# Turning two more tiles with VectorE, and moving turns and splits within their steps, in a two-layer linear-attention and MLP kernel

## The chip, the cores and the metric

The kernel runs on one core of a Trainium2 chip. A core has five engines with a queue each: TensorE (PE in the profile, with its weight loads as PEld), VectorE (DVE), ScalarE (ACT), GpSimd (POOL) and SyncE (SP). Each works through its own instructions in the order in which they were issued; semaphores make one wait for another. Here SP issues nearly all DMAs, so its queue is the order of the transfers. The metric is the device time of one execution in microseconds.

## The reference

The input x has 2048 rows of 448 numbers, all in float32. Two layers are applied, with the same weights. Each is a linear attention block (16 heads of 28) followed by an MLP with a hidden width of 1792:

```
phi = lambda t: where(t > 0, t + 1, exp(t)) + 1e-6
for layer in range(2):
    q, k, v = split(layernorm(x) @ wqkv)
    kv  = einsum("bhsd,bhse->bhde", phi(k), v)
    z   = phi(k) summed over the rows
    o   = (phi(q) @ kv) / (phi(q) . z + 1e-6)        # per head
    x   = x + o @ wo
    x   = x + gelu(layernorm(x) @ w1 + b1) @ w2 + b2
```

## The kernel before, in words

**Precision.** A float32 product is made of three products of halves: every operand is split into a high part (a cast) and a low part (the rest). hi x hi, hi x lo and lo x hi are accumulated in PSUM. A cast on ScalarE makes the high part, and VectorE or GpSimd subtracts to get the low part.

**Phase 1 of a layer** runs over 16 tiles of 128 rows, one step per tile. Around step t TensorE does, in this order: the K product of tile t (`proj`, L337, 11 matmuls of 128x448 into `psk`), the transposes of tile t+1 where TensorE makes them (L262, four into `tp`), the G product of tile t-1 (`stage_g`, L592, 11 matmuls, which gather phi(k) times x) and, in steps 2 to 8 of layer 0, the Q product of tile t (L337, `psq`). Of layer 0's other Q products, two are made ahead of the steps and seven behind them. From step 9 on a step has no Q product.

**Two ways to transpose.** K and Q need the normalised tile with its columns on the partitions, split into `XH` and `XL`. Way one: TensorE transposes into PSUM (`stage_b`), ScalarE casts from there (L274) and VectorE subtracts (L275). For the odd 64 columns at the end of such a tile ScalarE first copies them twice (L430, into spare space in `b2b`). Way two, the "turned" tiles: VectorE transposes in blocks of 32 (`turn`, L301 and L302) into half of a square `sq`; when the second tile of a pair is done, SP stores the square to DRAM (L307), and four DMAs bring it back spread as wanted (`spread`, L313, into `sp`). Then ScalarE casts from `sp` to `XH` (L319) and VectorE subtracts, from SBUF (`split_t`, L320). `TURNED` holds the first turned tile of each layer: 8 in layer 0, so tiles 0 to 7 go the first way there; in layer 1 all are turned.

**The order of a step** is written out by hand as tokens, in `STEP` for most steps and `STEPS` for others. Every engine gets its instructions in that order:

- `qp`: phi of the last Q product: two ScalarE activations (L353, L354), one VectorE operation (L356), and the store of the result to DRAM by SP (L565)
- `K`, `T`, `G`, `Q`: TensorE's products and the transposes of tile t+1
- `X`: the split of tile t+1 into `XH` and `XL` (ScalarE, then VectorE)
- `s`: the split of the normalised tile t for G (ScalarE cast L461; GpSimd L462 and L463)
- `a`, `aN`: layer norm's statistics of tile N (VectorE L207, L219, L212), and the power -0.5 on GpSimd (L213)
- `n`, `nN`: the normalisation of tile N (VectorE L426), which needs that power
- `kp`, `kh`, `kl`: phi of K (ScalarE, then VectorE L356), its high part (ScalarE L501), its low part and the running sum `za` (VectorE L510, L517)
- `tu`, `vN`: the turn of a tile, and the store if it ends a pair
- `bg`: in layer 0, the MLP's weights: SP loads pieces (L101 to L104, L392), and of pieces loaded earlier ScalarE casts the high part (L384, L387, L395) and GpSimd makes the low part (L385, L388, L396), up to two pieces a step until step 7, one later
- `ld`: SP loads later tiles of x (L85); `sp`: SP issues the spreads of all squares stored so far

The plain `a`, `n` and `tu` take their tile from `NORM`. Its row for step 5 is tile 10, for step 6 tile 11, for step 7 tile 12 and for step 8 tile 13.

The squares, the spread tiles and some weight pieces share five buffers of 128x1024, given out in turn. `k_at`, `q_at` and `g_at` say at which places among the 11 matmuls of a product those stand that read a low part of the tile: (2, 5, 8, 11) in K means that the second matmul already reads `XL`.

**Behind phase 1** a short transition forms the 448x448 matrix of the attention, and four MLP blocks of four tiles follow.

Of the kernel before, what the change touches and what calls it, by code (L numbers as in the profile page):

```python
# [22 lines left out]
def linear_attn_mlp_kernel(  # L23
# [12 lines left out]
    pe, act, dve, pool, sp = nc.tensor, nc.scalar, nc.vector, nc.gpsimd, nc.sync  # L36
# [8 lines left out]
    G = 112  # L45
# [37 lines left out]
    def load_x(l, t):  # L83
        xt[l, t] = t448("H", 8, f"x{l}_{t}")
        sp.dma_start(xt[l, t], x_d[l][t * 128:(t + 1) * 128, :])  # L85
# [164 lines left out]
    def block(key):  # L250
        if key not in blocks:
            blocks[key] = Block(APART if key[0] == "a" else 0)
        return blocks[key]
# [3 lines left out]
    def transpose_x(xn, tail, key, j, tag="m"):  # L257

        block(key)
        tp = tps[key, j] = bank(tag, 4 if tag == "acc" else 2, "tp")  # L260
        for c in range(4):
            pe.transpose(tp[:, c * 128:(c + 1) * 128], xn[:, c * 128:(c + 1) * 128] if c < 3 else tail, ident)  # L262
# [8 lines left out]
    def split_x(key, j):  # L271
        tp = tps.pop((key, j))
        hi, lo = blocks[key].pieces(j)
        act.copy(hi, tp)  # L274
        dve.tensor_sub(lo, tp, f(hi))  # L275
# [20 lines left out]
    def turn(x, key, t):  # L296
        x = x[:, :D]
        if (key, t // 2) not in squares:
            squares[key, t // 2] = half("sq")
        sq = squares[key, t // 2].rearrange("p (m c u n) -> p c m u n", m=4, c=4, n=32)[:, :, :, t % 2]  # L300
        dve.transpose(sq[:, :3], x[:, :TL].rearrange("p (c m n) -> p c m n", c=3, n=32))  # L301
        dve.transpose(sq[:, 3].rearrange("p (u m) n -> p u m n", u=2),  # L302
                      x[:, TL:].rearrange("p (m n) -> p m n", n=32)[:, None].to_broadcast([128, 2, 2, 32]))
# [56 lines left out]
    def bg_pieces():  # L360
        n = 0
        both = []

        def stage():
            nonlocal n
            n += 1
            if n <= LATE:
                k = (n - 1) // 2
                if k % 2 == 0 or k > 5:
                    return t512("xn", 2, "stg")[:, :D]  # L370

                if n % 2:
                    both.append(half("stg"))
                return both[-1][:, n % 2 * 512:][:, :D]
            return t448(f"W{5 + n % 2}", 1, "stg")

        for fc in range(4):
            sl = slice(fc * D, (fc + 1) * D)
            for c in range(4):
                s = stage_piece(w1[:, sl], c, sp, stage())  # L380

                def go(c=c, s=s, sl=sl):
                    if c < 3:
                        act.copy(w1h[:, c, sl], s)  # L384
                        pool.tensor_tensor(w1l[:, c, sl], s, f(w1h[:, c, sl]), op=OP.subtract)  # L385
                    else:
                        act.copy(w1x[:, sl], s)  # L387
                        pool.tensor_tensor(w1x[64:128, sl], s[64:128], f(w1x[64:128, sl]), op=OP.subtract)  # L388
                yield go
        for i in range(NF):  # L390
            s = stage()
            sp.dma_start(s, w2[i * 128:(i + 1) * 128, :])  # L392

            def go(i=i, s=s):
                act.copy(w2h[:, i], s)  # L395
                pool.tensor_tensor(w2l[:, i], s, f(w2h[:, i]), op=OP.subtract)  # L396
            yield go

    bg = bg_pieces()
# [14 lines left out]
    sts = {}  # L414


    TURNED = (8, 0)
    tails = {}

    def stage_a(l, t):  # L420
# [2 lines left out]
    def stage_n(l, t):  # L423
# [3 lines left out]
        xns[l, t] = xs  # L427
        if t < TURNED[l]:
            d = tails[l, t] = b2b[:, t % 2 * 128:][:, :128]
            act.copy(d.rearrange("p (u n) -> p u n", u=2), xs[:, None, TL:].to_broadcast([128, 2, 64]))  # L430

    def stage_t(l, t):
        if t >= TURNED[l]:
            turn(xns[l, t], ("a", l, t // 4), t % 4)
            if t % 2:
                store_sq(("a", l, t // 4), t % 4 // 2)

    def stage_sp(l, t):
        if t >= TURNED[l]:
            block(("a", l, t // 4))  # L440
            spread(("a", l, t // 4), t % 4 // 2)

    def stage_b(l, t, tag="h"):
        if t < TURNED[l]:
            transpose_x(xns[l, t], tails.pop((l, t)), ("a", l, t // 4), t % 4, tag)
# [4 lines left out]
    def stage_x(l, t):  # L450
        key = ("a", l, t // 4)
        if t < TURNED[l]:
            split_x(key, t % 4)
# [13 lines left out]

    def k_at(l, t):
        if t < 9:
            return (3, 6, 9, 11) if t == 0 or l == 0 and 2 < t < 8 else (2, 5, 8, 11)  # L470
        return (2, 5, 8, 11) if t == 9 else (1, 4, 7, 10)

    def q_at(l, t):
        if t < 9:
            return (2, 5, 8, 11) if l == 0 and t < 7 else (2, 4, 7, 10) if t == 0 else (1, 4, 7, 10)
        return {11: (4, 7, 10, 11), 12: (5, 7, 9, 11),
                13: (5, 8, 10, 11), 15: (1, 5, 8, 11)}.get(t, (1, 4, 7, 10))

    def g_at(l, t):
        if t < 9:  # L480
            return (4, 7, 10) if l == 0 and 0 < t < 6 else (3, 6, 9)
        return (2, 5, 8) if t < NT - 1 else (2, 6, 9)

    def stage_k(l, t, cs=range(4)):
        ko[l, t] = proj("k", ("a", l, t // 4), t % 4, ko.get((l, t)), cs, k_at(l, t))
# [47 lines left out]
    def stage_q(l, t, cs=range(4), tag=None):  # L533
        if tag:
            qs_[l, t] = bank(tag, 4, "psq")[:, :D]
        qs_[l, t] = proj("q", ("a", l, t // 4), t % 4, qs_.get((l, t)), cs, q_at(l, t))
        if 3 in cs:
            qo.append((l, t, qs_.pop((l, t))))
# [19 lines left out]
    def stage_qphi(n=9):  # L558
        for _ in qo[:n]:
            l, t, o = qo.pop(0)  # L560
            if (l, t) == (0, 0):
                by_rs(o)

            e = phi(o, "eq", tag="e" if t < NT - 2 else "E")
            sp.dma_start(pq_d[l][t * 128:(t + 1) * 128, :], e)  # L565

    def fill_qphi():

        l, t, o = qo.pop(0)
        e = t512("e", 3, "eq")[:, :D]  # L570
        p = t512("E", 2, "ep")[:, :D]
        act.activation(e, o, AF.Relu, scale=-1.0)
        act.activation(p, o, AF.Relu)
        act.activation(e, e, AF.Exp, scale=-1.0)
        pool.tensor_tensor(e, p, e, op=OP.add)
        sp.dma_start(pq_d[l][t * 128:(t + 1) * 128, :], e)

    def stage_g(l, t, acc, mid=lambda: None):
        h, lo = split.pop((l, t))
        kh, kl = ks.pop((l, t))  # L580
        first, last = t == 0, t == NT - 1
        x = [h[:, c * 128:(c + 1) * 128] for c in range(3)] + [h[:, TL:]]
        his = [(c, x[c], k) for c in range(4) for k in (kh, kl)]
        if t == NT - 3:
            his = his[::2] + his[1::2]
        los = [(c, lo[:, c * 128:(c + 1) * 128], kh) for c in range(3)]
        made = merge(his, los, g_at(l, t))
        for i, (c, w, k) in enumerate(made):
            if i == 3:
                mid()  # L590
            others = [m[0] for m in made[:i]], [m[0] for m in made[i + 1:]]
            pe.matmul(acc[c], w, k, start=first and c not in others[0], stop=last and c not in others[1])  # L592
# [20 lines left out]
    STEPS = {  # L613
# [9 lines left out]
    }  # L623
# [123 lines left out]
    def trans_gt(tr, acc):  # L747
        tr.gt = []
        for c in range(4):
            s = t512("A" if c < 2 else "B", 2, "gt")[:, :D]  # L750
            act.copy(s, acc[c])
            tr.gt.append(s)
# [52 lines left out]
    def load_pq(l, b, j):  # L805
        t = b * 4 + j
        pqt[l, t] = t448(f"W{j}", 1, f"pq{l}_{t}")
        sp.dma_start(pqt[l, t], pq_d[l][t * 128:(t + 1) * 128, :])
# [259 lines left out]
    for l in range(LAYERS):  # L1068
# [11 lines left out]
        def pre(j):  # L1080
# [6 lines left out]
            Q=lambda j: stage_q(l, fill.pop(0)), Qp=lambda j: fill_qphi(), Qv=lambda j: stage_qphi(j or 9),  # L1087
            Qa=lambda j: stage_q(l, fill.pop(0), tag="acc"), G=lambda j: stage_g(l, NT - 1, acc, lambda: trans_z(tr, zs[l])),
            ld=lambda j: (load_pq(l, 0, j), load_x(l, j)), gt=lambda j: trans_gt(tr, acc),
# [14 lines left out]
        for b in range(NB):  # L1104
# [6 lines left out]
            for i in range(NF):  # L1111
# [12 lines left out]
                elif l + 1 < LAYERS:  # L1124
# [4 lines left out]
                    if i in (3, 4, 6, 7, 8):  # L1129
                        t = (3, 4, 6, 7, 8).index(i)  # L1130
# [36 lines left out]
```

## Time and profile before

| | |
|---|---|
| median of 3 runs | 867.03 us (866.88 to 867.56) |
| the profiled execution | 866.72 us, its span 865.0 us |
| TensorE busy | 860.0 us, 99% of the span |
| VectorE, ScalarE, GpSimd busy | 57%, 40%, 24% |
| layer 0, step 3 (26.25 to 33.42) | VectorE 5.96 of 7.17 us |
| layer 0, step 4 (33.42 to 40.47) | VectorE 6.33 of 7.05 us |
| layer 0, step 5 (40.47 to 47.52) | VectorE 6.79 of 7.05 us |
| layer 0, step 8 (61.19 to 67.79) | VectorE 5.11 of 6.60 us |

A row of a timeline gives the start of an instruction from the span's start, its duration, engine, line, operation, what it writes and reads with shapes, and, where the engine was idle just before it, for how long and what ended that. Rows of one engine can overlap by some hundredths of a microsecond up to a tenth, because an instruction begins while the last one drains; so the pace of an engine is the difference of two starts. The matmul rows are pipelined as well, which is why the view of the chain, where pieces are joined end to end, is used for TensorE. Of step t, "start" is the start of its K product. SPq rows are the issues of DMAs.

### The profile page before, as it was taken

To read this page: it belongs to the slowest core of one execution; us is meant where nothing else is said; L and a number is where in the kernel's file an instruction comes from. 1 tells how busy PE (TensorE), PEld (TensorE's weight loads), DVE (VectorE), ACT (ScalarE), POOL (GpSimd) and SP (SyncE) were. 2 spreads that over 40 slices of the span, in tenths; PEclk is the share of its full clock that TensorE was granted. 3 is DMA by queue.
4 is the path that set the end of the run, shared out by engine and by line. 5 is a ranking of instruction groups with operands and counts; after the bars stand their busy time and mean duration, and the time that the engine had idled before them with its cause. 6 is when DMAs were issued, how large, how long until landed. Compare 5 with 4: busy or idle time off the path is not lost.

```text
span 865.0 us, 11662 instructions
## 1 busy us (share of the span) xinstructions
PE 860.0 (99%) x4181; PEld 770.6 (89%) x4181; DVE 494.6 (57%) x966; ACT 346.5 (40%) x606; POOL 211.1 (24%) x243
## 2 busy tenths in 40 slices
PE   9999999999999999999999999999999999999998
PEld 8999988888888888888899998988888888888887
DVE  7888596559456443236477876864674383533112
ACT  7776635333323322333356565433232233233231
POOL 3665612235013012012222343120220140140000
PEclk9999999999999999999999999999999999999999
DMA  5385536533313402051145433252332413111001
GB/s 171 128 248 174 183 90 216 183 112 108 134 61 117 147 0 98 1 182 49 49 152 185 163 130 108 103 187 80 117 109 88 139 72 112 50 49 43 0 1 43
DMA packets 63642, 94.76 MB, mean 110 GB/s; under 512 B 8928, under 2 KB 58720, under 8 KB 63584
## 3 DMA queue, kind: packets, MB, share of 16 engines
q1 hardware_dynamic: 63408, 93.87, 33.0%
q8 instruction: 33, 0.54, 0.3%
q14 instruction: 25, 0.20, 0.1%
q10 hardware_dynamic: 176, 0.14, 0.0%
HBM read 56.17 MB, written 34.60 MB: 105 GB/s over the span
## 4 chain that ended last, share of the span: by engine, by line
PE 99%; DVE 0%; issue 0%; ACT 0%; DVEq 0%
PE hp L924 32%; PE y L954 10%; PE y L953 10%; PE y L955 10%; PE G L592 8%; PE psq L337 8%; PE psk L337 8%; PE op L862 2%; PE op L861 2%; PE op L863 2%; PE op L851 1%; PE op L850 1%; PE op L852 1%; PE kvp L759 1%; PE mp L769 1%; PE psk L551 1%
## 5 line engine op out<-in xcount | busy, mean ns | idle before, releaser
L930 DVE TENSOR_TENSOR gl<-g,gh 128x512 fp32r<-128x512 f32 x112 | 83.2, 743 | 293.8 <-ACT gh L929 293.8
L926 ACT ACTIVATE g<-hp,b1s 128x512 f32<-128x512 f32 x112 | 77.4, 691 | 399.6 <-PE hp L924 398.8
L954 PE MATMUL y<-w2l,gh 128*128 128x448 f32 x447 | 163.6, 366 | 0.0
L953 PE MATMUL y<-w2h,gh 128*128 128x448 f32 x447 | 162.0, 362 | 0.0
L955 PE MATMUL y<-w2h,gl 128*128 128x448 f32 x447 | 160.1, 358 | 0.0
L924 PE MATMUL hp<-XH,w1h 128*128 128x512 f32 x336 | 130.7, 389 | 0.0
L924 PE MATMUL hp<-XH,w1l 128*128 128x512 f32 x336 | 130.7, 389 | 0.0
L924 PE MATMUL hp<-XL,w1h 128*128 128x512 f32 x336 | 130.1, 389 | 0.0
L213 POOL TENSOR_TENSOR brs<-bve,mhalf 128x1 f32<-128x1 f32 x63 | 39.3, 623 | 286.0 <-DVE bve L212 285.5
L953 PEld LDWEIGHTS y<-w2h,gh 128*128 128x128 f32 x447 | 83.7, 187 | 9.4
L954 PEld LDWEIGHTS y<-w2l,gh 128*128 128x128 f32 x447 | 83.9, 188 | 7.0
L955 PEld LDWEIGHTS y<-w2h,gl 128*128 128x128 f32 x447 | 84.0, 188 | 5.2 <-DVE gl L930 0.2
L924 PEld LDWEIGHTS hp<-XL,w1h 128*128 128x128 f32 x336 | 63.1, 188 | 13.1
L924 PEld LDWEIGHTS hp<-XH,w1h 128*128 128x128 f32 x336 | 63.0, 187 | 10.7
L924 PEld LDWEIGHTS hp<-XH,w1l 128*128 128x128 f32 x336 | 63.1, 188 | 9.9
L929 ACT CAST gh<-g 128x512 fp32r<-128x512 f32 x112 | 70.1, 626 | 3.5
L337 PE MATMUL psk<-wk,XH 128*128 128x448 f32 x210 | 61.8, 364 | 0.0
L337 PE MATMUL psq<-wq,XH 128*128 128x448 f32 x210 | 61.3, 366 | 0.0
L812 POOL TENSOR_TENSOR pz<-pq,zb 128x448 f32<-128x448 f32 x32 | 36.9, 1154 | 90.5 <-DVE dn L818 59.1
L462 POOL TENSOR_TENSOR xnl<-x,xnh 128x384 fp32r<-128x384 f32 x32 | 34.8, 1088 | 70.0 <-ACT xnh L461 56.7
L592 PE MATMUL G<-kh,xnh 128*128 128x448 f32 x128 | 46.8, 368 | 0.0
L592 PE MATMUL G<-kl,xnh 128*128 128x448 f32 x128 | 46.0, 365 | 0.0
(161 smaller groups left out, 1481.7 us busy)
## 6 DMA issues: line engine op xcount, KB each, us to landing
x<-in_A_x_dram SPq DMA_DIRECT2D x32, 224.0 KB, 3.7
pq_d<-eq SPq DMA_DIRECT2D x32, 224.0 KB, 2.7
pq<-pq_d SPq DMA_DIRECT2D x32, 224.0 KB, 3.2
sq_m<-sq SPq DMA_DIRECT2D x14, 512.0 KB, 2.8
sp<-sq_m SPq DMA_DIRECT2D x56, 128.0 KB, 2.8
x<-x_d SPq DMA_DIRECT2D x32, 224.0 KB, 3.5
sq_a<-sq SPq DMA_DIRECT2D x12, 512.0 KB, 2.9
sp<-sq_a SPq DMA_DIRECT2D x48, 128.0 KB, 2.8
```

The lines of the kernel that those rows point to most:

```text
L213: pool.tensor_tensor(rs, ve, mhalf, op=OP.pow)
L337: pe.matmul(o, x, p, start=(i == 0), stop=(i == 10))
L462: pool.tensor_tensor(lo[:, :TL], xn[:, :TL], f(h[:, :TL]), op=OP.subtract)
L592: pe.matmul(acc[c], w, k, start=first and c not in others[0], stop=last and c not in others[1])
L812: pool.tensor_tensor(pz, pqt[l, b * 4 + j], tr.zb, op=OP.mult)
L924: pe.matmul(o, w, r, start=(k == 0), stop=(k == len(made) - 1))
L926: act.activation(g, hp, AF.Gelu_apprx_tanh, bias=b1s[:, i:i + 1])
L929: act.copy(gh, g)
L930: dve.tensor_sub(gl, g, f(gh))
L953: pe.matmul(acc[j], gh[:, s], w2h[:, i], start=first, stop=False)
L954: pe.matmul(acc[j], gh[:, s], w2l[:, i], start=False, stop=False)
L955: pe.matmul(acc[j], gl[:, s], w2h[:, i], start=False, stop=stop)
```

## The change

In layer 0 tiles 6 and 7 are turned as well, so the tiles from 6 on take the way through `sq` and `sp`. Their turns stand in step 3. Step 3 loses the statistics of tile 8 and gets the normalisations of 6 and 7 (6 alone before); step 4 does the statistics of 8 and 9, the normalisation of 8 and the turn of 8; the normalisation and the turn of 9 stand at the head of step 5, and the turns of 10 to 14 at the head of steps 6 to 10 rather than late in steps 5 to 9. In steps 5 to 8, X stands behind kl rather than ahead of s; in step 5 the normalisation of 10 stands behind X. The tokens for spreads move with the stores: they stand at the end of steps 3, 5, 7, 9 and 10 (4, 6, 8 and 10 held work before). The places of the low matmuls in K, Q and G change for a few tiles.

```diff
-    TURNED = (8, 0)
+    TURNED = (6, 0)
...
     def k_at(l, t):
         if t < 9:
-            return (3, 6, 9, 11) if t == 0 or l == 0 and 2 < t < 8 else (2, 5, 8, 11)
+            return (3, 6, 9, 11) if t == 0 or l == 0 and 2 < t < 6 else (2, 5, 8, 11)
         return (2, 5, 8, 11) if t == 9 else (1, 4, 7, 10)
 
     def q_at(l, t):
         if t < 9:
-            return (2, 5, 8, 11) if l == 0 and t < 7 else (2, 4, 7, 10) if t == 0 else (1, 4, 7, 10)
+            return (2, 5, 8, 11) if l == 0 and t < 5 else (2, 4, 7, 10) if t == 0 else (1, 4, 7, 10)
...
     def g_at(l, t):
         if t < 9:
-            return (4, 7, 10) if l == 0 and 0 < t < 6 else (3, 6, 9)
+            return (4, 7, 10) if l == 0 and 0 < t < 4 else (3, 6, 9)
...
     STEPS = {
         (0, 1): "T X a3 q1 s kh n3 kl q1 G bg ld",
         (0, 2): "K T X s a4 kp n4 a5 kh kl n5 a6 G bg Q ld",
-        (0, 3): "qp K T X s a7 kp kh n6 kl a8 G bg Q ld",
-        (0, 4): "qp K T X s a9 kp kh n7 n8 kl n9 v8 v9 G bg Q ld sp",
-        (0, 8): "qp K T X s a kp n kh kl tu a14 G bg Q ld sp",
-        (0, 9): "qp K T X s kp n14 kh kl v14 G bg",
-        (0, 10): "K T X s a15 kp n15 kh kl v15 G bg sp",
+        (0, 3): "qp K T X n6 s a7 kp kh n7 v6 v7 kl G bg Q ld sp",
+        (0, 4): "qp K T X s a8 kp kh n8 a9 kl v8 G bg Q ld",
+        (0, 5): "qp K n9 v9 s a10 kp kh kl X n10 G bg Q ld sp",
+        (0, 6): "qp v10 K s a11 kp n11 kh kl X G bg Q ld",
+        (0, 7): "qp v11 K s a12 kp n12 kh kl X G bg Q ld sp",
+        (0, 8): "qp v12 K s a13 kp n13 kh kl X a14 G bg Q ld",
+        (0, 9): "qp v13 K X s kp n14 kh kl G bg sp",
+        (0, 10): "K v14 X s a15 kp n15 kh kl v15 G bg sp",
         (0, 11): "K T X kp s kh kl G bg",
         (1, 0): "K T X s kp kh kl a n tu Q ld sp",
     }
```

The steps without an entry of their own (5, 6 and 7 of layer 0 before) follow `STEP = "qp K T X s a kp n kh kl tu G bg Q ld sp"`.

## The prediction

> **What bounds the kernel now.** I read the page's busy shares and its chain first, then the chain in order of time for the first 220 us, and then the timelines of ScalarE (ACT), VectorE (DVE) and GpSimd (POOL) around the steps that change.
>
> ```profile
> span 865.0 us, 11662 instructions
> PE 860.0 (99%) x4181; PEld 770.6 (89%) x4181; DVE 494.6 (57%) x966; ACT 346.5 (40%) x606; POOL 211.1 (24%) x243
> ...
> PE 99%; DVE 0%; issue 0%; ACT 0%; DVEq 0%
> ```
>
> TensorE is the chain, so only two things move the end: matmul time taken away, and waits put into TensorE's stream. Step 4 of layer 0 and the start of step 9, in the chain's order (start, us, what):
>
> ```profile
> 33.42 2.21 PE psk L337 x11
> 35.63 0.44 PE tp L262 x4
> 36.06 2.21 PE G L592 x11
> 38.27 2.20 PE psq L337 x11
> ...
> 67.79 2.20 PE psk L337 x11
> ```
>
> A step is the K product (2.21 us), the next tile's four transposes (0.44), the G product of the tile before (2.21) and the Q product (2.20), with no gap: 7.06 us, or 6.61 without transposes. One matmul is 2.2 / 11 = 0.20.
>
> **Removed.** Tiles 6 and 7 lose their transposes: 2 x 0.44 = 0.88 us of TensorE, all of it on the path. Nothing else in the change can gain: two short ScalarE tail copies go, off the path. 0.88 us is 0.10% of 867.03, and 0.2% (1.73 us) is about what a measurement of this kernel can tell from no change. So the question is how much waiting comes in.
>
> **Prices of one step.** The rows of step 9 (K product 67.79 to 69.99) give the shortest loop from one product to the next:
>
> ```profile
> 67.89 0.55 ACT L353 ACTIVATE eq<-psq 128x448 f32<-128x448 f32 x1 [1.51 <-PE psq L337]
> 68.47 0.58 ACT L354 ACTIVATE eq<-eq 128x448 f32<-128x448 f32 x1
> ...
> 70.03 0.55 ACT L353 ACTIVATE ek<-psk 128x448 f32<-128x448 f32 x1
> 70.61 0.58 ACT L354 ACTIVATE ek<-ek 128x448 f32<-128x448 f32 x1
> 71.89 0.64 ACT L501 ACTIVATE kh<-psk,tiny 128x448 fp32r<-128x448 f32 x1 [0.70 <-DVE psk L356]
> 72.42 0.56 ACT L384 CAST w1h<-stg 128x448 fp32r<-128x448 f32 x1
> 72.88 0.62 ACT L319 CAST XH<-sp 128x512 fp32r<-128x512 f32 x1
> 73.40 0.57 ACT L461 CAST xnh<-x 128x448 fp32r<-128x448 f32 x1
> ```
>
> ```profile
> 62.96 0.69 DVE L320 TENSOR_TENSOR XL<-sp,XH 128x512 fp32r<-128x512 f32 x1
> ...
> 71.22 0.63 DVE L356 SCALAR_TENSOR_TENSOR psk<-psk,ek 128x448 f32<-128x448 f32 x1
> 71.76 0.50 DVE L426 TENSOR_SCALAR x<-x,bmv,brs 128x448 f32<-128x448 f32 x1
> 72.56 0.62 DVE L510 SCALAR_TENSOR_TENSOR kl<-psk,kh 128x448 fp32r<-128x448 f32 x1 [0.29 <-ACT kh L501]
> 73.10 0.61 DVE L517 TENSOR_TENSOR za<-psk,za 128x448 f32<-128x448 f32 x1
> ```
>
> ```profile
> 73.06 1.16 POOL L385 TENSOR_TENSOR w1l<-stg,w1h 128x448 fp32r<-128x448 f32 x1 [0.61 <-ACT w1h L384]
> ```
>
> From end of K: ek 0.04 later, the k phi on VectorE (L356) 1.23 after, kh 0.67 after its start, kl 0.67 after kh's start, za 0.54 after kl. So kh starts 4.10 after K's start. VectorE moves on 0.54 after a phi, a kl or a za.
>
> **Added on VectorE.** Two turns in step 3, and their pace:
>
> ```profile
> 42.17 0.57 DVE L301 STREAM_TRANSPOSE sq<-x 128x384 f32<-128x384 f32 x1
> 42.66 0.27 DVE L302 STREAM_TRANSPOSE sq<-x 128x128 f32<-128x128 f32 x1
> 42.85 0.53 DVE L301 STREAM_TRANSPOSE sq<-x 128x384 f32<-128x384 f32 x1
> ```
>
> One turn is 42.85 - 42.17 = 0.68. They stand ahead of kl(3), together with the normalisations of 6 and 7, where there was one normalisation. Rows of step 3 now, and of a normalisation that met GpSimd:
>
> ```profile
> 31.23 1.02 POOL L462 TENSOR_TENSOR xnl<-x,xnh 128x384 fp32r<-128x384 f32 x1
> 32.55 0.55 POOL L213 TENSOR_TENSOR brs<-bve,mhalf 128x1 f32<-128x1 f32 x1
> ```
>
> ```profile
> 19.91 1.20 DVE L426 TENSOR_SCALAR x<-x,bmv,brs 128x448 f32<-128x448 f32 x1
> 21.03 0.61 DVE L510 SCALAR_TENSOR_TENSOR kl<-psk,kh 128x448 fp32r<-128x448 f32 x1
> ...
> 31.38 0.62 DVE L207 BATCH_NORM_STATS2 bst<-x 128x6 f32<-128x448 f32 x1
> ...
> 32.32 0.62 DVE L356 SCALAR_TENSOR_TENSOR psk<-psk,ek 128x448 f32<-128x448 f32 x1
> ```
>
> ```profile
> 19.84 1.02 POOL L462 TENSOR_TENSOR xnl<-x,xnh 128x384 fp32r<-128x384 f32 x1
> ```
>
> Statistics of a tile take 32.32 - 31.38 = 0.94. A normalisation alone takes 0.50; at 19.91, begun 0.07 after a GpSimd split, it took 1.20 and VectorE moved on 1.12 later. In the changed step 3, n6 comes where the statistics stood, at 31.38, 0.15 after the split at 31.23: it waits likewise. Walk: n6 to 32.5, statistics of 7 to 33.45, phi 34.0, GpSimd's power (0.55) 34.1, n7 34.6, two turns 35.95, kl(3) done 36.6. G(3) starts at 36.06 and its second matmul, at 36.26, reads kl(3): **a wait of 0.4** (between 0, if n6 doesn't meet the split, and 0.8, if the power is later by as much; I take the rows' own order). So step 5 starts 0.4 late, at 40.86.
>
> **Moved: the splits of turned tiles.** In steps 5 to 8 X goes behind kl: ScalarE's XH then starts 0.53 after kh (72.42 - 71.89), the weight piece's cast 0.52 after that (73.40 - 72.88), and GpSimd's split of that piece 0.64 after the cast (73.06 - 72.42): 1.69 after kh. VectorE's XL comes at 0.67 (kl) + 0.54 (za) + 0.53 = 1.74 after kh. The two start 0.05 apart, GpSimd first. What then happens is seen in layer 1, where the same kl, za and XL meet a GpSimd split at the same lead:
>
> ```profile
> 503.00 0.61 DVE L517 TENSOR_TENSOR za<-psk,za 128x448 f32<-128x448 f32 x1
> 503.53 1.52 DVE L320 TENSOR_TENSOR XL<-sp,XH 128x512 fp32r<-128x512 f32 x1
> ```
>
> ```profile
> 503.49 1.02 POOL L462 TENSOR_TENSOR xnl<-x,xnh 128x384 fp32r<-128x384 f32 x1 [2.72 <-ACT xnh L461]
> ```
>
> XL, begun 0.04 behind GpSimd, took 1.52 in place of 0.69 and ended 0.54 after GpSimd's end (505.05 against 504.51). Behind a 1.16 us split it would end 1.69 + 1.16 + 0.54 = 3.39 after kh's start; alone it ends at 1.74 + 0.69 = 2.43. K of the next tile needs it as its second matmul.
>
> The Trainium skill (SBUF — State Buffer, "Who interferes with whom") says that a VectorE instruction with two SBUF inputs contends with a GpSimd instruction that reads SBUF, that the one which issues first holds the shared pair for the whole instruction, and that with at most one SBUF input VectorE doesn't contend. The 1.52 at 503.53 agrees. But by that rule the order of issue decides, and a start time in a row isn't that order to 0.05 us: with VectorE first the sum is that of the first rival below.
>
> **Walk of steps 4 to 9.** Step 4 on VectorE: za(3) till 37.05, phi(3) and the split of 5 (PSUM) 38.2, statistics of 8 39.15, phi(4) 39.7, n8 40.2, statistics of 9 41.15, kl(4), za 42.25, turn of 8 42.95. G(4) starts 43.06: no wait. Step 5: q phi 43.5; n9 meets GpSimd's splits of pieces 4 and 5 (casts till 41.9, then tile 9's power and two splits of 1.16: till 44.1), so 44.5; turn of 9 45.2; statistics of 10 46.15; k phi 46.15, kh 46.82, XH(6) 47.35 to 47.97, XL(6) from 48.56. Q(5) ends at 40.86 + 6.61 = 47.47, so K(6) would read XL at 47.67. Behind GpSimd (from 48.51) XL ends at 46.82 + 3.39 = 50.2: **a wait of 2.6**. Step 6: K ends 52.3; n10 meets the split of piece 7 (50.1 to 51.2) and ends at 51.6; q phi, the turn of 10 and the statistics of 11 last to 53.75; k phi 53.75, kh 54.42, XL(7) ends 57.8; Q(6) ends 56.7, K(7) would read it at 56.9: **0.95**. Step 7: K ends 59.86, phi 61.1, kh 61.76, XL(8) ends 65.15 against 64.47 (as second matmul): **0.7**. Step 8: the statistics of 14 stand after X and ahead of the weight piece in GpSimd's order, so XL(9) is alone: kh + 2.43 = 67.21 - 2.20 + 4.10 + 2.43 = 71.54 against 71.82, no wait.
>
> **Moved: turns, stores, spreads.** The SP queue's rows now:
>
> ```profile
> 43.61 0.33 SPq L307 DMA_DIRECT2D sq_a<-sq  x1
> ...
> 46.56 1.76 SPq L313 DMA_DIRECT2D sp<-sq_a  x4
> ```
>
> ```profile
> sp<-sq_a SPq DMA_DIRECT2D x48, 128.0 KB, 2.8
> ```
>
> A spread is issued 2.95 after its store and its last piece lands some 1.3 + 2.8 later, in all 7.1 after the turn. Added: one store and four spread pieces; step 3's two weight loads and tile 10 queue behind the store (36.0) and land by about 41.5, so the casts of step 4 wait some 0.3, hidden. Tiles 6 and 7 land at 43.1 and are wanted at 47.35. The store of 12 and 13 (v13 at about 74.1) lands 81.2, XL(12) is due at 84.8: hidden by 3.6. That of 14 and 15 lands 90.7 against 93.6 less 1.3 for the split: 1.6 left; without that cover each us late is a us lost. The other orders of the low matmuls in K, Q and G keep their counts: nothing but the earlier need of XL counted above. Buffers: piece 11 takes the spread of 6 and 7, free at 57.8; SP waits there, tile 13's load and the q store behind it, which nothing wants before 66.
>
> **Sum.** 0.4 + 2.6 + 0.95 + 0.7 - 0.88 = +3.8 us. The profiled execution took 866.72 us for a span of 865.0, and becomes 870.5; the median of the three runs, 867.03, stands 0.31 above it, and becomes 870.8.
>
> **Rivals.** (1) VectorE first: if GpSimd starts even a little after XL (its lead of 0.05 is made of six rounded differences), XL(6) ends at 46.82 + 2.43 = 49.25, wait 1.6, and those of 7 and 8 vanish: 0.4 + 1.6 - 0.88 = +1.1, 868.2, not told from no change. For it: the smallness of the lead. Against: at 0.04 GpSimd already won, and whatever delays kl widens the lead. (2) All hidden, 867.03 - 0.88 = 866.15: XL(6) would have to end 1.6 sooner than even alone. n6 and n9 unhindered would give 0.7 + 0.5, which leaves 0.4 wanting, and the split at 31.23 speaks against the first. (3) Only XL(6) waits for GpSimd: 0.4 + 2.6 - 0.88 = +2.1, 869.2. (4) The store and the spread of 14 and 15 take 1.5 longer each than in the rows, because more of them now fall together: 3.0 less the cover of 1.6, so +1.4 more, 872.2; against it, the rows above kept 2.95 and 2.8 beside weight loads.
>
> **How the numbers follow.** Forecast 0.60; rival 1 0.20; all hidden 0.07; only XL(6) 0.06; late spreads 0.07. Slower by over 0.2% (above 868.76): 0.60 + 0.06 + 0.07 = 0.73. Within: 0.20 and most of 0.07, 0.25. Faster by over 0.2% would need twice the transposes' time: 0.02. The likeliest case alone, with G's wait from 0 to 0.8 and a locked XL between 1.50 and 1.65: 869.9 to 871.7. The range goes down to rival 1 with its own G bound and up to rival 4: 867.7 to 872.4, leaving out some 0.1.
>
> **What would show it.** Right: tp groups lose 8 matmuls; PE waits appear at K(6), K(7), K(8) on XL L320 and at G(3) on kl; XL of 6 to 8 lasts 1.5 to 1.7. Wrong: XL of 0.69 there (rival 1), or no PE wait ahead of 48 us (rival 2).

## The result and the profile after

The changed kernel takes 872.24 us (median, 871.48 to 872.55) against 867.00 of the kernel before (866.88 to 867.56): a ratio of 1.0060, with an interval of 1.0047 to 1.0073. It is 5.2 us slower. The profiled execution took 872.15 us for a span of 870.4, against 866.72 and 865.0.

The page of the kernel after, busy times and shares of the chain:

```profile
span 870.4 us, 11662 instructions
...
PE 862.3 (99%) x4173; PEld 771.5 (89%) x4173; DVE 498.4 (57%) x970; ACT 344.2 (40%) x604; POOL 211.5 (24%) x243
...
PE 94%; DVE 3%; issue 1%; POOL 1%; ACT 0%; DMA 0%; DVEq 0%; POOLq 0%
```

TensorE has 8 matmuls fewer (4173 against 4181) and is busy 2.3 us longer. Its share of busy time still reads 99%; its share of the chain fell from 99% to 94%. The waits of TensorE in the kernel after (us in total, times, longest):

```profile
PE psk L337 <- DVE XL L320: 2.5, 2, 1.8
...
PE psk L337 <- ACT XH L319: 0.5, 1, 0.5
PE G L592 <- DVE kl L510: 0.2, 1, 0.2
```

The rows where they lie, in TensorE's timeline of the kernel after:

```profile
35.84 0.45 PE L592 MATMUL G<-kh,xnh 128*128 128x448 f32 x1
36.53 0.47 PE L592 MATMUL G<-kl,xnh 128*128 128x448 f32 x1 [0.24 <-DVE kl L510]
36.84 0.36 PE L592 MATMUL G<-kh,xnh 128*128 128x448 f32 x1
...
47.26 0.36 PE L337 MATMUL psq<-wq,XH 128*128 128x448 f32 x1
48.16 0.47 PE L337 MATMUL psk<-wk,XH 128*128 128x448 f32 x1 [0.54 <-ACT XH L319]
50.38 0.61 PE L337 MATMUL psk<-wk,XL 128*128 128x448 f32 x1 [1.75 <-DVE XL L320]
...
54.08 0.37 PE L592 MATMUL G<-kh,xnh 128*128 128x448 f32 x1
...
65.12 0.37 PE L337 MATMUL psk<-wk,XH 128*128 128x448 f32 x1
66.21 0.47 PE L337 MATMUL psk<-wk,XL 128*128 128x448 f32 x1 [0.72 <-DVE XL L320]
```

A matmul row shows 0.36 us, but the next one starts 0.20 later; what goes beyond 0.20 from start to start is lost. The time in brackets is less than that, because the row before lasts 0.16 us or more beyond the usual start of the next. So read, G(3) loses 0.49, of which 0.40 is the wait (its first two matmuls are also 0.09 apart without one), K(6) 0.70 and 2.02, K(8) 0.89. After the waits at G(3) and K(8) the first matmul takes 0.47 rather than 0.36 and the next one starts 0.11 late. I call these 0.11 a refill; what happens in them no row shows. K(7) doesn't wait.

The largest surprise stands between 50.38 and 54.08: ten matmuls of K(6) took 3.70 us, where ten take 2.0. Windows of the kernel after (length, busy time of PE, PEld, DVE, ACT and POOL, then the granted clock, DMA share, GB/s):

```profile
50.00:51.00 1.00, 0.61 (x2) 0.57 (x3) 1.00 (x2) 0.55 (x2) 1.00 (x1) 0.78 0.66 239
51.00:52.00 1.00, 1.00 (x4) 0.88 (x4) 1.00 (x2) 0.00 (x0) 1.00 (x2) 0.50 0.81 251
52.00:53.00 1.00, 1.00 (x4) 0.92 (x3) 1.00 (x4) 0.00 (x0) 0.72 (x2) 0.50 0.73 229
53.00:54.00 1.00, 1.00 (x4) 0.89 (x3) 0.64 (x3) 0.00 (x0) 0.21 (x1) 0.51 0.97 280
54.00:55.00 1.00, 1.00 (x6) 0.94 (x6) 0.00 (x0) 0.69 (x2) 0.33 (x1) 1.00 0.82 287
```

Right after the wait TensorE was granted half its clock. What is missing from full clock sums to 0.22 + 0.50 + 0.50 + 0.49 = 1.71 us, the 1.70 that the ten matmuls took too long; at a half each, that is some 3.4 us of half clock (estimated from these windows).

The ledger: -0.88 (transposes) + 0.40 + 0.11 (G(3) and its refill) + 2.72 (K(6)) + 1.70 (half clock, its refill included) + 0.89 + 0.11 (K(8)) = +5.05. The MLP's first product starts at 140.32 against 135.14, +5.18; the span grew by 5.4.

### The profile page after: what moved, and what is told of

It is laid out like the page before. It is cut to its first block, busy times and chain, and to the rows that moved or that the text cites. A ratio compares the mean times of both kernels' runs of the same rounds, so it can differ in the third digit from the quotient of the medians.

```text
span 870.4 us, 11662 instructions
## 1 busy us (share of the span) xinstructions
PE 862.3 (99%) x4173; PEld 771.5 (89%) x4173; DVE 498.4 (57%) x970; ACT 344.2 (40%) x604; POOL 211.5 (24%) x243
## 4 chain that ended last, share of the span: by engine, by line
PE 94%; DVE 3%; issue 1%; POOL 1%; ACT 0%; DMA 0%; DVEq 0%; POOLq 0%
PE hp L927 32%; PE y L957 10%; PE y L956 10%; PE y L958 10%; PE G L592 7%; PE psk L337 7%; PE psq L337 6%; PE op L865 2%; PE op L864 2%; PE op L866 2%; PE op L854 1%; PE op L853 1%; PE op L855 1%; PE kvp L762 1%; PE mp L772 1%
## 5 line engine op out<-in xcount | busy, mean ns | idle before, releaser
L320 DVE TENSOR_TENSOR XL<-sp,XH 128x512 fp32r<-128x512 f32 x54 | 46.5, 869 | 2.2 <-ACT XH L319 2.1
```

Source lines behind the costliest of these rows:

```text
L320: eng.tensor_tensor(lo.rearrange("p (c i n) -> p c i n", c=4, n=32), x, f(h), op=OP.subtract)
```

## The experiments

What makes the XL of tiles 6 and 8 late is seen in VectorE's and GpSimd's timelines of the kernel after:

```profile
48.71 1.62 DVE L320 TENSOR_TENSOR XL<-sp,XH 128x512 fp32r<-128x512 f32 x1
...
57.87 0.68 DVE L320 TENSOR_TENSOR XL<-sp,XH 128x512 fp32r<-128x512 f32 x1
...
64.51 1.64 DVE L320 TENSOR_TENSOR XL<-sp,XH 128x512 fp32r<-128x512 f32 x1
```

```profile
48.65 2.68 POOL L385 TENSOR_TENSOR w1l<-stg,w1h 128x448 fp32r<-128x448 f32 x2 [1.63 <-ACT w1h L384]
...
57.87 1.70 POOL L388 TENSOR_TENSOR w1x<-stg,w1x 64x448 fp32r<-64x448 f32 x1 [3.54 <-ACT w1x L387]
...
64.45 2.71 POOL L385 TENSOR_TENSOR w1l<-stg,w1h 128x448 fp32r<-128x448 f32 x2 [1.74 <-ACT w1h L384]
```

Where GpSimd's split began 0.06 sooner, XL took 1.62 and 1.64. Where both began at 57.87, XL took 0.68 and GpSimd's split 1.70 in place of the 1.16 it takes alone. The first four experiments start from the kernel after; each changes what stands there. "Measured" gives the median, its ratio to the kernel before as it ran beside the experiment (867.01 us in these four) with the 95% interval, and the span of the profiled execution.

**X back at the head of the steps.** Only the place of X changes in steps 5 to 8 (and in step 5 that of the turn of 9 behind it):

```diff
-        (0, 5): "qp K n9 v9 s a10 kp kh kl X n10 G bg Q ld sp",
-        (0, 6): "qp v10 K s a11 kp n11 kh kl X G bg Q ld",
+        (0, 5): "qp K X n9 v9 s a10 kp kh kl n10 G bg Q ld sp",
+        (0, 6): "qp v10 K X s a11 kp n11 kh kl G bg Q ld",
...
```

> Steps 5 to 8 of the changed kernel with X back ahead of s, all else as changed (tiles 6 and 7 still turned). Theory A (X behind kl is what makes K(6) and K(8) wait): both waits and the slow stretch at 50 us go, the wait at G(3) stays: span 865.0 - 0.88 + 0.4 = 864.5 us, against 870.4 of the changed kernel and 865.0 before. Rival B (the two more turns overload VectorE wherever X stands): XL(6) still ends near 49 us, K(6) still waits over 1 us, span 868 or more.

Measured: 870.44 us, 1.0039 (1.0024 to 1.0054), span 868.6. Neither theory fits: 1.8 us less than after, but still 3.4 above before. The waits at K(6) and K(8) and the half clock are gone. Other waits came. VectorE's timeline of this kernel around step 5:

```profile
45.12 0.69 DVE L320 TENSOR_TENSOR XL<-sp,XH 128x512 fp32r<-128x512 f32 x1 [1.47 <-ACT XH L319]
...
49.91 0.62 DVE L510 SCALAR_TENSOR_TENSOR kl<-psk,kh 128x448 fp32r<-128x448 f32 x1 [0.70 <-ACT kh L501]
```

The XH it waits for waits itself, until 44.47, for the spread of tiles 6 and 7, which the walk had there at 43.1. kl(5) comes at 49.91, where it came at 47.64 after, and G(5) waits for it. Later XLs now meet GpSimd at the head of the step, and TensorE's timeline shows K(10) waiting:

```profile
74.69 0.47 PE L337 MATMUL psk<-wk,XL 128*128 128x448 f32 x1 [1.56 <-DVE XL L320]
```

So the place of X alone isn't the cause; with the turns at the head as well, X is late there too.

**Statistics behind X.** The statistics of 11, 12 and 13 go behind X, so that GpSimd's queue is held and XL starts clear of its split:

```diff
-        (0, 5): "qp K n9 v9 s a10 kp kh kl X n10 G bg Q ld sp",
-        (0, 6): "qp v10 K s a11 kp n11 kh kl X G bg Q ld",
+        (0, 5): "qp K n9 v9 s a10 kp kh kl X n10 a11 G bg Q ld sp",
+        (0, 6): "qp v10 K s kp n11 kh kl X a12 G bg Q ld",
...
```

> The statistics of tiles 11, 12 and 13 move one step up, behind X, as those of 14 stand already, so that in GpSimd's order the weight pieces' splits come behind a power that waits for VectorE, and XL of 6, 7 and 8 meets no GpSimd split. Theory A (GpSimd's split holds XL up by 0.93 us where it starts first): XL(6) takes 0.69 and ends at 49.4 rather than 50.33, K(6)'s second matmul waits 1.75 rather than 2.7, K(8) doesn't wait; span 870.4 - 0.95 - 1.2 = 868.2, and down to 866.4 if the shorter idle also leaves TensorE at full clock. Rival B (VectorE's queue alone sets XL's end): waits within 0.3 us of the changed kernel's, span 870 or more.

Measured: 869.60 us, 1.0031 (1.0019 to 1.0043), span 867.7. The timelines of VectorE, GpSimd and TensorE in this kernel:

```profile
48.76 0.68 DVE L320 TENSOR_TENSOR XL<-sp,XH 128x512 fp32r<-128x512 f32 x1
```

```profile
51.40 2.27 POOL L385 TENSOR_TENSOR w1l<-stg,w1h 128x448 fp32r<-128x448 f32 x2
```

```profile
47.31 0.36 PE L337 MATMUL psq<-wq,XH 128*128 128x448 f32 x1
48.21 0.47 PE L337 MATMUL psk<-wk,XH 128*128 128x448 f32 x1 [0.54 <-ACT XH L319]
49.49 0.47 PE L337 MATMUL psk<-wk,XL 128*128 128x448 f32 x1 [0.81 <-DVE XL L320]
```

On GpSimd the power for tile 11 now stands ahead of the split and waits for those statistics, so the split starts at 51.40 rather than 48.65. XL(6) starts 0.05 from where it did (48.71) and takes 0.68: 0.94 us less, and K(6)'s second matmul comes 0.89 sooner. That is the price of GpSimd's lead. K(6) still loses 0.70 + 1.08, and the clock stays full. With a full clock theory A had 866.4. Part of the 1.3 above that is seen: the normalisations of 11 and 12 now meet GpSimd (1.34 and 1.16 us rather than 0.50), the kl and XL behind them are late, and K(7) and K(8) lose 0.39 and 0.20, with a refill each.

**TensorE kept busy through the wait.** Fourteen matmuls of weights by weights go ahead of K(6), into the bank that K(6) then overwrites (another bank than before):

```diff
+                    if (l, t) == (0, 6):
+                        o = bank("m", 2, "psb")[:, :D]
+                        ko[0, 6] = o
+                        for _ in range(14):
+                            pe.matmul(o, wkq["k", 0][0][:, :128], wkq["k", 0][0], start=True, stop=True)
```

> Fourteen useless matmuls (2.8 us, into the PSUM bank that K(6) then overwrites) stand ahead of K(6), so that TensorE is busy while it waits for XL(6). Theory A (the ten matmuls behind the wait took 3.86 us rather than 2.0 because the clock fell to half after the idle time): they take 2.0, the granted clock stays 1.00 from 48 to 55 us, span 870.4 - 1.9 = 868.5 although work was added. Rival B (they are slow because DMA traffic or VectorE and GpSimd disturb them): still some 3.9 us, span 870.4.

Measured: 870.97 us, 1.0047 (1.003 to 1.0064), span 869.1: work was added and the kernel became 1.3 us faster than after. The chain of this kernel, and the window in which the clock had begun to fall before:

```profile
47.69 2.84 PE psb L711 x14
50.52 2.25 PE psb L337 x11
```

```profile
50.00:51.00 1.00, 1.00 (x6) 0.82 (x5) 1.00 (x2) 0.62 (x2) 1.00 (x1) 1.00 0.64 217
```

The clock stays at 1.00, and K(6) takes 2.25 for 11 matmuls. XL(6) is as late as before. So the 1.7 us belong to TensorE's idling itself, not to the late data or to what the other engines and the DMAs did then. The gain is 1.3 rather than 1.7. K(6)'s second matmul starts at 50.56 rather than 50.38, behind the added matmuls, which is 0.2 of the difference; the rest wasn't traced.

**kl(3) ahead of the turns.** G(3)'s wait of 0.4 should go:

```diff
-        (0, 3): "qp K T X n6 s a7 kp kh n7 v6 v7 kl G bg Q ld sp",
+        (0, 3): "qp K T X n6 s a7 kp kh kl n7 v6 v7 G bg Q ld sp",
```

> In step 3 kl stands ahead of n7, v6 and v7. The wait of 0.4 us at G(3) goes. If the terms of the sum add (as the prediction had it): span 870.4 - 0.4 = 870.0. If the wait at G(3) was swallowed by the longer one at K(6), because VectorE's queue has hardly a gap from 30 to 47 us and sets the end of XL(6) whatever TensorE did before: XL(6) ends within 0.1 us of where it did, K(6)'s wait grows by 0.4, span 870.4.

Measured: 875.07 us, 1.0094 (1.0079 to 1.0109), span 873.7: 2.8 us slower than after, which neither of the two cases had. The turn of 7 ends later, and so does the store behind it. The chain of this kernel in step 3 has that store (SPq L307), a weight load behind it on SP and the cast that waits for the load:

```profile
38.05 0.33 SPq L307
...
39.71 3.89 DMA stg<-in_B_w_dram
43.62 0.57 ACT w1h L384
```

The walk had the store at 36.0; here it stands at 38.05. On ScalarE the cast stands ahead of the phi of Q. ScalarE's timeline of this kernel, and that of the kernel after at the same cast:

```profile
43.62 0.57 ACT L384 CAST w1h<-stg 128x448 fp32r<-128x448 f32 x1 [1.16 <-DMA stg<-in_B_w_dram]
```

```profile
40.89 0.57 ACT L384 CAST w1h<-stg 128x448 fp32r<-128x448 f32 x1 [0.16 <-DMA stg<-in_B_w_dram]
```

The cast starts 2.7 us later than in the kernel after, and all behind it on ScalarE with it; TensorE waits for XH(6) as well, and the clock halves (TensorE's waits and the chain of this kernel):

```profile
PE psk L337 <- ACT XH L319: 2.8, 1, 2.8
```

```profile
52.75 4.01 PE psk L337 x10
```

**The parts one at a time.** The other four start from the kernel before. The kernel before took 866.70 us beside them. The places of the low matmuls (`k_at`, `q_at`, `g_at`) are those of the kernel after in all four. First, tiles 6 and 7 turned, at the end of step 3 and behind kl; the order of all steps from 5 on is as before:

```diff
-    TURNED = (8, 0)
+    TURNED = (6, 0)
...
-        (0, 3): "qp K T X s a7 kp kh n6 kl a8 G bg Q ld",
-        (0, 4): "qp K T X s a9 kp kh n7 n8 kl n9 v8 v9 G bg Q ld sp",
+        (0, 3): "qp K T X s a7 kp kh n6 kl n7 v6 v7 G bg Q ld sp",
+        (0, 4): "qp K T X s a8 a9 kp kh n8 kl n9 v8 v9 G bg Q ld",
```

> Tiles 6 and 7 turned by VectorE at the end of step 3 (behind kl), tile 8's statistics in step 4, and every other step in the order of the kernel before: X early, turns late. Theory A (the turning costs nothing, the moves of X, kl and the turns do): no wait over 0.2 us in the K and G products, the 0.88 us of transposes come back: span 865.0 - 0.9 = 864.1, median 866.1 against 867.0 of the kernel before. XH(6) waits for the spread: the store is issued at about 37.1 and in the run with X early the spread was there 8.5 us after the store, so 45.6, and XL(6) ends 1.3 later at 46.9, 0.4 before K(6) reads it. Rival B (two more turns overload VectorE): XL(6) or kl comes later than that, waits of 1 us or more, span 866 or more.

Measured: 866.39 us (865.83 to 867.57) against 866.70 (866.5 to 867.57) of the kernel before beside it, 0.9996 (0.9987 to 1.0005): not told apart from before. Each set against the kernel before beside it, this is 5.5 us under after (0.3 under, against 5.2 over). The profiled execution, the shortest of its eleven, has a span of 864.1. There the MLP's first product starts at 134.12 against 135.14 before, and 0.12 of that was there ahead of G(3): 0.90 less behind it, the 0.88 of the transposes. Why the median gains only 0.3 wasn't traced. From step 3 to the MLP the chain of this kernel is TensorE alone (start, us):

```profile
44.76 2.20 PE psq L337 x11
46.96 2.20 PE psk L337 x11
49.16 2.22 PE G L592 x11
```

Second, that kernel with X behind kl in steps 5 to 8 and nothing else moved:

```diff
+        (0, 5): "qp K s a10 kp n10 kh kl X v10 G bg Q ld sp",
+        (0, 6): "qp K s a11 kp n11 kh kl X v11 G bg Q ld sp",
+        (0, 7): "qp K s a12 kp n12 kh kl X v12 G bg Q ld sp",
+        (0, 8): "qp K s a13 kp n13 kh kl X v13 a14 G bg Q ld sp",
```

> The kernel f1 with X behind kl in steps 5 to 8 and nothing else. Theory A: XL(6) starts 0.05 behind GpSimd's split, K(6) waits some 2, K(7) and K(8) up to 0.9 each (where GpSimd wins): span 864.1 + 2 + 0.9 to 1.8 = 867.0 to 867.9, and 1.7 more if the wait at K(6) is long enough to halve the clock. Rival B (X's place is harmless, it was VectorE's backlog from step 3): span within 0.5 of f1.

Measured: 869.67 us, 1.0035 (1.0021 to 1.0048), span 868.1. That is 3.3 over the turn alone by the medians, and 4.0 by the profiled executions, of which that of the turn alone was its shortest. TensorE's timeline of this kernel:

```profile
46.62 0.36 PE L337 MATMUL psq<-wq,XH 128*128 128x448 f32 x1
47.54 0.47 PE L337 MATMUL psk<-wk,XH 128*128 128x448 f32 x1 [0.56 <-ACT XH L319]
48.82 0.47 PE L337 MATMUL psk<-wk,XL 128*128 128x448 f32 x1 [0.81 <-DVE XL L320]
...
56.46 0.47 PE L337 MATMUL psk<-wk,XL 128*128 128x448 f32 x1 [0.75 <-DVE XL L320]
...
64.08 0.47 PE L337 MATMUL psk<-wk,XL 128*128 128x448 f32 x1 [0.73 <-DVE XL L320]
```

0.72 + 1.08 at K(6), 0.92 at K(7), 0.91 at K(8) and three refills of 0.11 make the 4.0. GpSimd holds up only XL(8) here (1.65); XL(6) and XL(7) took 0.68 and are late because they stand behind kl. The expectation had XL(6) behind GpSimd's split; so K(6)'s 1.8 came by another way than the 2 that it gave.

Third, the turn alone with the turns of 10 to 14 at the head of the next steps, X as before:

```diff
+        (0, 5): "qp K X s a10 kp n10 kh kl G bg Q ld sp",
+        (0, 6): "qp v10 K X s a11 kp n11 kh kl G bg Q ld",
...
+        (0, 9): "qp v13 K X s kp n14 kh kl G bg sp",
+        (0, 10): "K v14 X s a15 kp n15 kh kl v15 G bg sp",
```

> The kernel f1 with the turns of 10 to 14 at the head of the next step (X stays early) and nothing else. Theory A from the run with X early: the turn and XL stand between the q phi and the k phi on VectorE, XL there starts behind GpSimd's split of xn and takes 1.2 to 1.4, so kl is late (waits of 0.1 to 0.5 at G) and XL(10) misses the short step 9 (1.7 at K(10)): span 864.1 + 2.5 = 866.6. Rival B (the turns' place is harmless): within 0.5 of f1.

Measured: 869.50 us, 1.0029 (1.0018 to 1.004), span 868.1: 3.1 over the turn alone by the medians, and again 4.0 by the profiled executions. Behind a turn at the head of the step X meets GpSimd's split (1.36 or 1.37 us for XL in steps 6 to 8, 1.24 in step 9). VectorE's and TensorE's timelines of this kernel:

```profile
73.01 1.24 DVE L320 TENSOR_TENSOR XL<-sp,XH 128x512 fp32r<-128x512 f32 x1
```

```profile
72.36 0.37 PE L592 MATMUL G<-kl,xnh 128*128 128x448 f32 x1
74.30 0.47 PE L337 MATMUL psk<-wk,XL 128*128 128x448 f32 x1 [1.58 <-DVE XL L320]
```

K(10) loses 1.74 of the 4.0. The rest lies in small gaps at G products and K(12); they weren't traced further.

Last, the moves without the turning: the first turned tile stays 8, tiles 6 and 7 keep TensorE's transposes (T in steps 5 and 6), all else is the order of after:

```diff
+        (0, 3): "qp K T X n6 s a7 kp kh n7 v6 v7 kl G bg Q ld sp",
+        (0, 4): "qp K T X s a8 kp kh n8 a9 kl v8 G bg Q ld",
+        (0, 5): "qp K T n9 v9 s a10 kp kh kl X n10 G bg Q ld sp",
+        (0, 6): "qp v10 K T s a11 kp n11 kh kl X G bg Q ld",
...
```

Here v6 and v7 do nothing, since tiles 6 and 7 aren't turned.

> The changed kernel's order of steps, but tiles 6 and 7 still transposed by TensorE (T stands in steps 5 and 6; v6 and v7 fall away). Theory A (the moves alone cost): XL(6) and XL(7) read PSUM, which GpSimd's split doesn't hold up, but stand behind kl, so K(6) waits about 1; ScalarE's tail copy of n6, which meets GpSimd's split, delays G(3) by up to 1; XL(8) is held up by 0.9 at K(8): span 865.0 + 2 to 3 = 867 to 868. Rival B (the turning is what costs): span 865 to 865.5.

Measured: 871.85 us, 1.0054 (1.0041 to 1.0068), span 870.4, that of after. Its TensorE timeline and chain at K(6), where XL comes from PSUM (L275):

```profile
47.38 0.36 PE L337 MATMUL psq<-wq,XH 128*128 128x448 f32 x1
48.66 0.47 PE L337 MATMUL psk<-wk,XH 128*128 128x448 f32 x1 [0.92 <-ACT XH L274]
49.98 0.51 PE L337 MATMUL psk<-wk,XL 128*128 128x448 f32 x1 [0.84 <-DVE XL L275]
```

```profile
49.98 3.86 PE psk L337 x10
```

The clock halved again (0.50 in the windows from 51 to 53 us), after gaps of 1.08 and 1.12; ten matmuls took 3.86 as the chain counts them, where it also has 3.86 after. The expectation, made without that term, was too low.

## Why the prediction held, point by point

The time was to be 870.8, and is 872.24. The direction came out, and so did the places but for K(7), and the mechanism that the prediction walked through; the sum was +3.8 against +5.2, as one term was missing. That the time lies inside the range of 867.7 to 872.4 is in part luck: the likeliest case alone was to go up to 871.7, and the rest of the range was there for late spreads (rival 4), which didn't come. The missing 1.70 of half clock took their place, and the 0.95 of K(7) that didn't come paid for part of it.

- **Transposes, -0.88:** confirmed by rows: 8 matmuls fewer, and 0.90 less from G(3) to the MLP in the profiled execution of the turn alone. Its median, 0.3 under before, can't be told from no gain.
- **G(3), 0.4:** confirmed, 0.40. n6 met GpSimd's split as the walk had it.
- **K(6), 2.6:** confirmed, 2.72 as gaps. XL(6) was to start at 48.56, 0.05 behind GpSimd at 48.51; it started at 48.71, 0.06 behind 48.65. Taking GpSimd's lead away gave back 0.89 of it; the rest is X standing behind a kl that comes late, as the first rival had it for the lone XL (a wait of 1.6; the runs show 1.78). The wait came in two parts, 0.70 for XH and 2.02 for XL. The walk had XH(6) end at 47.97, behind K(6)'s start at 47.47, but named only the wait for XL; its total is the same either way, but the matmul between the two matters below.
- **K(7), 0.95:** didn't come (the walk's own times give 0.9). XL(7) and GpSimd's split began together and VectorE went first, the first rival's mechanism at one tile. The kernel with TensorE kept busy repeats it with the clock full: equal starts at 56.41, XL 0.68, and no wait at K(7).
- **K(8), 0.7:** 0.89, with XL of 1.64 as foretold. **K(9), none:** confirmed.
- **A term was missing:** the step "K ends 52.3", which took ten matmuls at 0.20 behind a wait of 2.6. TensorE had lost its full clock by then, and they took 1.70 longer. That is the size of the whole difference between the span's +5.4 and the sum's +3.8; the absent K(7) (-0.95) is made up by K(6), K(8), two refills (0.11 each, also not counted) and the 0.35 between ledger and span, which I didn't trace.
- **"The casts of step 4 wait some 0.3, hidden":** 0.16 and hidden, but the cover was thin, as the kernel with kl(3) moved shows: a store 2 us later stopped ScalarE's queue.
- **Late spreads (rival 4) and all hidden (rival 2):** TensorE waits for no spread of 14 and 15, and it does wait at 36 us.

The Trainium skill (SBUF — State Buffer, "Who interferes with whom") says that issue order decides who holds the shared pair. The rows agree: 1.62 behind a split that began 0.06 sooner, 0.68 without one, and with equal starts GpSimd was the one that took longer, 1.70. It also exempts an instruction with one SBUF input outside VectorE's two-port modes, a condition that the prediction left out. The exemption agrees with the kernel of moves alone, where XL(7) from PSUM took 0.68 from 57.47 on, beside GpSimd's split that ran from 57.44 and took its usual 1.16. The condition matters: the normalisation, which reads one tile from SBUF, took 1.11 at 31.34 behind a GpSimd split from 31.18, and 0.51 without one. Whether it ran in such a mode no run here shows.

What the prediction didn't separate, and the parts alone show: in the old order turning two more tiles costs nothing that can be measured, and the loss comes with the moves. Each of the two moves of steps 5 to 9 alone costs 3.1 to 3.3 us by the medians (4.0 by the profiled executions), and all moves without the turning cost what the whole change does (+5.15 against +5.24). So in the new order the turning gains nothing either: its 0.88 go into the 0.51 at G(3), where the kernel of moves alone has no wait, and into K(6), which loses 2.72 there with the turning and 2.20 without. The two moves don't simply add up (8.0 against the 6.3 between the spans of the turn alone and after, though the 6.3 also hold the half clock and G(3)); that a TensorE which is already late waits less for the next late operand is an argument, not a measurement.

## What to carry to other kernels

An engine with 99% of the chain gains from removed work only if no operand comes later; before a split is moved, walk the queue in front of it to the first product that reads it. Price a wait of TensorE not by its own length alone: look at the granted clock in the stretch behind it. And when a change has several parts, run the one that removes the work by itself: here it was 5.5 us better than the whole.

## What the runs showed of the hardware that was not expected

- **Half clock after a wait below 3 us.** Gaps of 0.70 + 2.02 us around one matmul (after), 1.08 + 1.12 (moves alone) and 3.00 + 2.02 (kl(3) first) each brought half clock, and the ten matmuls took 3.7 to 3.9 us from start to start; 0.70 + 1.08 (statistics behind X), 0.72 + 1.08 (X late alone) and a single 1.74 (turns at the heads) did not. The Trainium skill (TensorE: Matmul & The Clock Gate, "Part 1: The HAM clock gate") has the clock either half or full, set by how busy TensorE was over free-running windows of some 3.4 us. The rows of 0.50 and the 3.4 us worked out above agree, and so do the two other kernels: windows of 0.2 us put the half clock from 50.57 to 53.98 after, give 3.4 us again in the moves alone, and in kl(3) first give 6.8, twice as much, from 49.71, within the wait, to 56.54. But the page's cold state follows an idle window, and here a matmul ran within the wait of after, and in kl(3) first the clock fell some 2.2 us into the gap. Where the limit lies between 1.8 and 2.2 us of idling, or whether the place of the wait in such a window decides, stays open.
- **A refill of 0.11 us** follows a wait of TensorE at full clock in the kernels here that have one: 36.53 to 36.84 where 0.20 is usual.
- **Two operations that contend and start at the same recorded time** went VectorE first, four times (57.87 after, 56.41 with TensorE kept busy, 60.39 with kl(3) first, 55.72 with X late alone). That is too few to call a rule, and all four are the same pair, XL(7) against the split of `w1x`. With GpSimd 0.04 to 0.06 ahead of XL, GpSimd went first each time: 48 such pairs in the ten traces, XL 1.50 to 1.66. So a lead of 0.05 in the rows was enough to tell here, which the prediction doubted.
